# The entry of a fused attention backward loop: square root as a power on GpSimd, the last shift rows and the stores of q moved into the loop

## The chip, the cores and the metric

The kernel runs on one core of one Trainium2 chip. The metric is the device time of one execution in microseconds (us), as a median over runs. The core has five engines that run their own instruction queues in order and meet through semaphores: TensorE (PE, with PEld for its weight loads), VectorE (DVE), ScalarE (ACT), GpSimd (POOL) and SyncE (SP). TensorE writes to PSUM banks, which DVE and ACT read. DMAs are issued from the queues of SP, ACT and POOL.

## The reference

Two attention blocks over 2048 tokens and 448 columns, and the gradients of both. Block A is linear attention, block B is multi-query attention: 16 query heads of 28 columns share one key and one value head. Cut to block B, which the change concerns:

```python
q = (x @ wq).reshape(B, S, H, Dh).transpose(0, 2, 1, 3)
k = x @ wk
v = x @ wv
scores = jnp.einsum("bhqd,bkd->bhqk", q, k) * (Dh ** -0.5)
p = _softmax(scores, axis=-1)
o = jnp.einsum("bhqk,bkd->bhqd", p, v)
return o.transpose(0, 2, 1, 3).reshape(B, S, H * Dh) @ wo
```

The kernel returns the outputs of both blocks (concatenated) and the gradients of x and of all weights, for a given gradient of the output.

## The kernel before, in words

**Stages.** `phase_A` computes block A, forward and backward, until about 192 us. `phase_B_pre` then projects q, k and v of block B until about 218 us. The core, the loop `for u in range(NU + 28)`, computes block B's attention forward and backward together until about 1004 us. A tail computes the weight and input gradients that are left.

**phase_B_pre.** q is kept transposed in `R1`: four groups of 128 rows, in each four heads of 32 rows (28 columns of q and 4 more), 2048 tokens along the row. Row 0 of each head's 32 rows holds a shift, by which the softmax is kept from overflowing: the square root of |q|² times the largest |k|². It multiplies a row of −1 in k, so the product of q and k gives the shifted score at once. The loop over `qc` (four chunks of 512 tokens) makes, per chunk, four groups of q (ScalarE copies them out of PSUM, L585; DVE squares them, L587), a product that sums the squares by head into one PSUM bank `pn` (16 rows), a `Sqrt` of that bank on ScalarE with the scale `kmax2` (L592), and four small DMAs from POOL's queue that put the 16 rows into `R1` (L594, here called puts). After every second chunk four DMA transposes on SP (L599) bring 1024 tokens of q into the order of tokens, and one DMA (L600, 1 MB) stores them to `qn_d` in DRAM, from where the core loads them as `qX` for its dk products.

**The core.** There are 64 blocks: 256 query tokens by two heads each. A block takes 8 units, and a unit u is 256 keys of one block. Unit u does, each with its own lag:

- the scores of unit u on TensorE (into the banks `SB`, three in rotation) and the dp products of unit u−16 (banks `DB`), `rows_SD`;
- two exps of the scores on ScalarE (L904, L944) into the exp tiles `eT`, and from unit 16 on ScalarE's copy `cp` of the second dp half (L911), DVE's product of the first (L909), POOL's product of the second (L912);
- after every fourth unit one DMA transpose of an exp tile (`eN`, 1 MB, L946) on SP; the dv products (`dv_mm`, u−20) read it. Block 0's dv products in unit 20 need the first two eN tiles, block 1's in unit 28 the next two;
- on even units the o and dq products (`o_dq`), on odd units the dk products (`dk_m`, u−27), which read `qX`;
- once per block a normalisation of o: unit 10 of the block has `prod`, `don` and a copy on POOL (L800 to L804), which TensorE transposes in unit 14 (`don_T`).

**The order of the work.** The core is written under a manual schedule: each engine's instructions stand in program order. Outside of it a scheduler may reorder. `do_proj` projects the gradient of the output through wo, 16 tiles of 128 tokens in two halves of 256 columns each. The table `do_slots` (L881) says in which unit which half is made: units 1 to 15 (into the `DB` banks, which are free until unit 16, with four products of 128x256), five odd units 17 to 25 (into `dk_acc`, free until unit 27), and every eighth unit from 32 to 120 (into a spare `SB` bank). Outside the `DB` banks each half is made of 16 products of 32 columns each. `do_copy` copies a half out on DVE (L879).

**PSUM and SBUF.** `phase_A` and `phase_B_pre` use one PSUM pool of eight banks (`aacc` and `agen`, four each); the core opens another. The core's SBUF pools lie in the memory that the pools of `phase_A` held, so the first writes of the core wait for the last readers there. The shift rows of the first three chunks lie in such memory (`ga`), the fourth in `R3`, which stays.

**Activation tables.** ScalarE holds one table of functions at a time. `Sqrt` and `Exp` are not in the same one: the program loads a table ahead of the first L592 and one ahead of a dummy exp of one column, `ex` (L883), at the head of the core.

Of the kernel before, what the change touches and what calls it, by code (L numbers as in the profile page):

```python
# [8 lines left out]
ACT = mybir.ActivationFunctionType  # L9
# [5 lines left out]
H = 16  # L15
DH = 28
D = 448
P = 128
# [7 lines left out]
def kernel(  # L26
# [50 lines left out]
    ex = cst.tile([P, 1], F32, name="ex")  # L77
    nc.vector.memset(ex[:], 0.0)
# [9 lines left out]
    def flat(t):  # L88
        return t.rearrange("p a b -> p (a b)")
# [34 lines left out]
    def phase_A(pa, cA, cB, awk, psA):  # L124
# [401 lines left out]
        return xbT, wq_pad, rep, bsel, gaB, ga[:, 8:12, :]  # L526

    def phase_B_pre(pa, cA, awk, psA, io):
        xbT, wq_pad, rep, bsel, qn, sh = io
# [41 lines left out]
        shifts = [flat(sh)[0:H, i * 512:(i + 1) * 512] for i in range(NQC - 1)] + [flat(R3)[0:H, 5120:5632]]  # L571
        kmax2 = cA.tile([H, 1], F32, name="kmax2")
        for qc in range(NQC):
# [17 lines left out]
            shift = shifts[qc]  # L591
            nc.scalar.activation(out=shift, in_=pn[0:H, :], func=ACT.Sqrt, scale=kmax2[:, 0:1])  # L592
            for g in range(4):
                nc.gpsimd.dma_start(qT[:, g, qs].rearrange("(j r) s -> j r s", r=32)[:, 0, :], shift[4 * g:4 * g + 4, :])  # L594
            if qc % 2:
                q2 = slice((qc - 1) * 512, (qc + 1) * 512)
                t2 = slice(4 * qc - 4, 4 * qc + 4)
                for g in range(4):
                    nc.sync.dma_start_transpose(qn[:, t2, g * P:(g + 1) * P], qT[:, g, q2])  # L599
                nc.sync.dma_start(qn_d[q2, :].rearrange("(t p) c -> p t c", p=P), qn[:, t2, :])  # L600
# [5 lines left out]
        nc.gpsimd.memset(vaug_[:, :, 0:1], 1.0)  # L606

# [3 lines left out]
    kn_ = R3f[:, 4608:5120].rearrange("p (t c) -> p t c", c=32)  # L611
    with ExitStack() as pa:
        psA = pa.enter_context(tc.tile_pool(name="psA", bufs=4, space=bass.MemoryType.PSUM))
# [4 lines left out]
        phase_B_pre(pa, cA, awk, psA, io)  # L618
# [5 lines left out]
    psc = ExitStack()  # L624
    with ExitStack() as cs_:
        psA = psc.enter_context(tc.tile_pool(name="psAcc", bufs=1, space=bass.MemoryType.PSUM))
# [9 lines left out]
        SB = [psA.tile([P, 512], F32, name=f"sps{i}") for i in range(3)]  # L636
        DB = [psA.tile([P, 512], F32, name=f"dps{i}") for i in range(2)]
        oq = psA.tile([P, 512], F32, name="oq")
        dv_acc = psA.tile([P, 512], F32, name="dv_acc")
        dk_acc = psA.tile([P, 512], F32, name="dk_acc")  # L640
# [220 lines left out]
        def dv_mm(b, h, qb):  # L861
# [6 lines left out]
        def do_proj(i, h, ps):  # L868
            if ps is DB[0] or ps is DB[1]:
                for c in range(4):  # L870
                    mm(ps[:, 0:256], gbT[:, i, c, :], woTp[:, c, h * 256:(h + 1) * 256], start=(c == 0), stop=(c == 3))
                return
            for c in range(4):
                for j in range(4):
                    js = slice(32 * j, 32 * j + 32)
                    mmt(ps[js, 0:256], gbT[:, i, c, js], woTp[:, c, h * 256:(h + 1) * 256], (0, 32 * j), c == 0, c == 3)

        def do_copy(i, h, ps):
            nc.vector.tensor_copy(out=do_nat[:, i, h * 256:(h + 1) * 256], in_=ps[:, 0:256])  # L879

        do_slots = {u: divmod(n, 2) for n, u in enumerate([*range(1, 16), *range(17, 27, 2), *range(32, 128, 8)])}  # L881
        with tc.manual_schedule():
            tc.keep_in_program_order(nc.scalar.activation(out=ex[:], in_=ex[:], func=ACT.Exp))  # L883
            for u in range(NU + 28):
# [14 lines left out]
                if dpj is not None:  # L899
                    dps_ = DB[u % 2] if u < 16 else dk_acc if u < 27 else spare  # L900
                    do_proj(*dpj, dps_)
# [189 lines left out]
```

## Time and profile before

Three runs took 1079.1, 1080.79 and 1082.69 us, a median of 1080.79. The profiled execution took 1080.88 us, with a span of 1079.1 us between its first and last instruction.

| engine | busy us of the span | share |
|---|---|---|
| TensorE (PE) | 1027.6 | 95% |
| DVE | 895.5 | 83% |
| ScalarE (ACT) | 876.7 | 81% |
| POOL | 772.1 | 72% |

| what | count | one, in us |
|---|---|---|
| exp of the scores, ACT L904 and L944 | 1024 | 0.61 to 0.63 |
| copy `cp`, ACT L911 | 512 | 0.61 |
| product of 128x512, POOL L912 | 512 | 1.16 |
| square root of 16x512, ACT L592 | 4 | 0.68 |
| put of 4 shift rows, POOL L594 (issue; landing) | 16 | 0.56; 1.9 and 2.7 |
| q transposes, SP L599 (issue) | 8 | 1.2 to 2.8 |
| load of qX, POOL (issue; landing) | 32 | 0.6; 4.3 |

A busy time is the sum over instructions of an engine. Start to start, two exps lie 0.49 us apart, less than their duration, since neighbours overlap. "x4" in a timeline merges four instructions that follow each other. A value in square brackets is the idle time of the engine just before an instruction, and behind the arrow is what ended it. DMA shares can be over 1, as they add what the packets of all queues took on the 16 DMA engines.

### The profile page before, as it was taken

What the parts mean: (1) busy time and instruction counts of PE and PEld (TensorE: products, weight loads), DVE (VectorE), ACT (ScalarE), POOL (GpSimd) and SP (SyncE); (2) the same over time, 40 slices, a digit from 0 to 9 for tenths busy, and PEclk for the clock granted to TensorE, in tenths of its full rate; (3) what the DMA queues carried; (4) which work ended last, traced back from release to release, by engine and by line L of the source; (5) the groups of instructions that cost most, each with busy time, mean ns of one, the idle gap of its engine ahead of it and who ended that gap; (6) DMA issues with size and microseconds to landing.
All of it is one profiled execution on the core that took longest, in us unless ns stands there. A gap on an engine that the chain in (4) does not pass through costs nothing.

```text
span 1079.1 us, 40135 instructions
## 1 busy us (share of the span) xinstructions
PE 1027.6 (95%) x16326; PEld 489.1 (45%) x16329; DVE 895.5 (83%) x1792; ACT 876.7 (81%) x1744; POOL 772.1 (72%) x1014
## 2 busy tenths in 40 slices
PE   9999999998999999999999999999999999999998
PEld 5555455443444444444444444444444444444434
DVE  7897400447999999999999999999999999999943
ACT  6463122577999999999999999999999999999622
POOL 6001243327888888888988888988998899888881
PEclk9999999998999999999999999999999999999999
DMA  9979899499999999999999999999999999999973
GB/s 239 165 131 195 161 196 193 88 215 169 202 210 198 179 190 187 197 188 201 183 187 191 201 188 194 204 184 182 193 203 186 193 194 193 196 177 180 221 140 92
DMA packets 669026, 199.36 MB, mean 185 GB/s; under 512 B 646008, under 2 KB 664736, under 8 KB 668840
## 3 DMA queue, kind: packets, MB, share of 16 engines
q1 hardware_dynamic: 656296, 175.23, 95.5%
q0 software_dynamic: 7584, 17.59, 6.9%
q10 hardware_dynamic: 4960, 3.96, 1.4%
q8 instruction: 128, 2.10, 0.8%
q14 instruction: 58, 0.48, 0.2%
HBM read 20.99 MB, written 12.94 MB: 31 GB/s over the span
## 4 chain that ended last, share of the span: by engine, by line
PE 34%; POOL 18%; ACT 18%; DVE 14%; issue 12%; DMA 4%; DVEq 0%; ACTq 0%; POOLq 0%; SPq 0%
POOL dsT L912 13%; PE agen L81 13%; ACT cp L911 9%; ACT eT L944 7%; DVE dsx L975 6%; PE sps L653 5%; PE aacc L81 4%; PE oq L653 4%; DVE dsT L909 3%; DMA eN<-eT 2%; PE dv_acc L653 2%; POOL prod L800 1%; PE dps L653 1%; DMA out_dram<-dsT 1%; DVE R L929 1%
## 5 line engine op out<-in xcount | busy, mean ns | idle before, releaser
L912 POOL TENSOR_TENSOR dsT<-cp,eT 128x512 bf16<-128x512 bf16 x512 | 588.4, 1157 | 104.5 <-ACT cp L911 98.6
L975 DVE STREAM_TRANSPOSE dsx<-dsT 128x512 f32<-128x512 f32 x512 | 357.7, 699 | 2.3 <-DVE R L723 0.2
L653 PEld LDWEIGHTS <-R 128*32 128x32 bf16 (+1 forms) x9184 | 229.5, 94 | 278.8 <-issue 238.7
L909 DVE TENSOR_TENSOR dsT<-dps,eT 128x512 bf16<-128x512 f32 x512 | 341.6, 667 | 16.5 <-PE dps L653 11.7
L904 ACT ACTIVATE eT<-sps 128x512 bf16<-128x512 f32 x512 | 312.6, 611 | 22.9 <-PE dps L653 10.7
L911 ACT ACTIVATE cp<-dps 128x512 bf16<-128x512 f32 x512 | 314.2, 614 | 12.0 <-PE dps L653 10.9
L944 ACT ACTIVATE eT<-sps 128x512 bf16<-128x512 f32 x512 | 320.3, 626 | 0.0
L653 PE MATMUL dk_acc<-dsx,qX 32*32 32x512 bf16 x4096 | 268.3, 376 | 0.0
L653 PE MATMUL dps<-doT,R 32*128 32x256 bf16 x2048 | 248.7, 270 | 1.9 <-ACT cp L911 0.8
L653 PE MATMUL sps<-R,R 32*128 32x256 bf16 (+1 forms) x2240 | 222.1, 274 | 7.6 <-DVE R L879 1.7
L653 PE MATMUL oq<-eT,R 128*32 128x256 bf16 x2048 | 158.3, 275 | 1.4 <-issue 1.4
L653 PE MATMUL oq<-dsT,R 128*32 128x256 bf16 x2048 | 157.1, 275 | 0.1
L653 PEld LDWEIGHTS <-qX 32*32 32x32 bf16 x4096 | 79.8, 89 | 114.4 <-issue 54.1
L653 PE MATMUL dv_acc<-eN,don 128*32 128x512 bf16 x1024 | 98.1, 381 | 3.8 <-DMA eN<-eT 3.8
L81 PEld LDWEIGHTS <-R 128*128 128x128 bf16 (+1 forms) x525 | 41.5, 98 | 41.7 <-issue 12.2
L406 POOL COPY pk<-R 128x256 bf16<-128x256 bf16 x4 | 1.6, 399 | 73.2 <-DVE R L366 73.1
L653 PEld LDWEIGHTS <-don 128*32 128x32 bf16 x1024 | 33.8, 97 | 5.0 <-issue 4.5
L422 DVE TENSOR_TENSOR osb<-aacc,pr 64x448 bf16<-64x448 f32 x2 | 1.2, 616 | 41.1 <-ACT pr L421 24.9
L800 POOL TENSOR_TENSOR prod<-R,oTs 128x128 f32<-128x128 bf16 x64 | 28.0, 438 | 7.7 <-DVE oTs L796 7.4
L929 DVE TENSOR_SCALAR R<-oq 64x256 bf16<-64x256 f32 x64 | 27.3, 427 | 3.6 <-PE oq L653 1.6
L817 PE MATMUL sps<-identB,don 128*32 128x128 bf16 x256 | 18.6, 224 | 12.3 <-POOL don L809 8.4
L81 PE MATMUL agen<-R,R 128*128 128x448 bf16 x128 | 28.6, 352 | 0.0
(232 smaller groups left out, 978.7 us busy)
## 6 DMA issues: line engine op xcount, KB each, us to landing
qX<-qn_d POOLq DMA_DIRECT2D x32, 256.0 KB, 4.3
out_dram<-osb ACTq DMA_DIRECT2D x22, 112.0 KB
qn_d<-gaT SPq DMA_DIRECT2D x2, 1024.0 KB
eN<-eT SPq DMA_TRANSPOSE x128
xa<-in_A_x_dram SPq DMA_DIRECT2D x8, 224.0 KB
ga<-in_grad_out_dram SPq DMA_DIRECT2D x4, 448.0 KB
xa<-in_grad_out_dram POOLq DMA_DIRECT2D x4, 448.0 KB, 12.2
out_dram<-wdq POOLq DMA_DIRECT2D x8, 224.0 KB, 6.3
```

What stands on the lines that cost most here:

```text
L81: nc.tensor.matmul(out_ap, lhsT=lhsT, rhs=rhs, start=start, stop=stop, tile_position=(0, 0))
L406: nc.gpsimd.tensor_copy(out=pk[:, t4, D:512], in_=gqn[:, t4, 3 * P:D])
L653: nc.tensor.matmul(out, lhsT=lhsT, rhs=rhs, start=start, stop=stop, tile_position=pos, skip_group_check=True)
L800: nc.gpsimd.tensor_tensor(out=prod[b][:], in0=dnv, in1=os_, op=ALU.mult)
L817: nc.tensor.transpose(tp2[q:q + 32, qb * P:(qb + 1) * P], don[b][:, qb, h, :], identB[:, :], tile_position=(0, q))
L904: nc.scalar.activation(out=eT(u)[:, 0, :], in_=sp[0][:, :], func=ACT.Exp, scale=scale)
L909: nc.vector.tensor_tensor(out=dst[:, 0, :], in0=dp[0][:, :], in1=ew[:, 0, :], op=ALU.mult)
L911: nc.scalar.activation(out=cp[:, :], in_=dp[1][:, :], func=ACT.Copy)
L912: nc.gpsimd.tensor_tensor(out=dst[:, 1, :], in0=cp[:, :], in1=ew[:, 1, :], op=ALU.mult)
L929: nc.vector.tensor_scalar(out=qT_B[g][64 * hp:64 * hp + 64, qc * 256:(qc + 1) * 256], in0=oq[64:128, 0:256], scalar1=scale, scalar2=None, ...
L944: nc.scalar.activation(out=eT(u)[:, 1, :], in_=sp[1][:, :], func=ACT.Exp, scale=scale)
L975: nc.vector.transpose(out=dsx[b][:, tp, :, :, :].rearrange("p h t c -> p (h t c)").bitcast(F32), in_=dsT[y][:, :, :].rearrange("p h c -> p ...
```

## The change

Four things are changed.

1. The square root: a new function `q_shift` scales the sums with an `Identity` on ScalarE (`kmax2`, and 1e-30 added) into a temporary, and raises that to the power 0.5 with a `tensor_tensor` on POOL. The dummy exp is gone. All three calls in `phase_B_pre` use the same temporary, `tmp[0]`.
2. `phase_B_pre` makes the shifts of the chunks 0 to 2 and puts those of 0 and 1. The fourth `q_shift` and the puts of the chunks 2 and 3 stand in the core after the first exp of unit 1. The second four q transposes stand at the core's head, ahead of these puts, so q goes to `qn_d` without its shift rows for the last 1024 tokens; the dk rows that these make are not used. Their 1 MB store from SP becomes four stores of 256 tokens (256 KB) from POOL, in units 34, 42, 50 and 58. The loads of `qX` for the second chunk of 256 tokens move to units 66 to 78, and the load of `wo` from unit 70 to 86.
3. The core's PSUM banks are tiles of the pool of `phase_A` (`aacc`, `agen`); the bank of the fourth sum stays in use until unit 1 and then becomes `dv_acc`.
4. `do_proj` makes 13 whole tiles of 512 columns with four products each in the odd units 1 to 25, and six halves in the units 32 to 72.

```diff
+    def q_shift(pn, shift, tmp):
+        a = tmp[0][0:H, :]
+        nc.scalar.activation(out=a, in_=pn[0:H, :], func=ACT.Identity, bias=eps[:, 0:1], scale=kmax2[:, 0:1])
+        nc.gpsimd.tensor_tensor(out=shift, in0=a, in1=half[:, 0:1].to_broadcast([H, 512]), op=ALU.pow)
+
+    def put_shift(shift, qs):
+        for g in range(4):
+            nc.gpsimd.dma_start(R1[:, g, qs].rearrange("(j r) s -> j r s", r=32)[:, 0, :], shift[4 * g:4 * g + 4, :])
...
-            shift = shifts[qc]
-            nc.scalar.activation(out=shift, in_=pn[0:H, :], func=ACT.Sqrt, scale=kmax2[:, 0:1])
-            for g in range(4):
-                nc.gpsimd.dma_start(qT[:, g, qs].rearrange("(j r) s -> j r s", r=32)[:, 0, :], shift[4 * g:4 * g + 4, :])
-            if qc % 2:
-                q2 = slice((qc - 1) * 512, (qc + 1) * 512)
-                t2 = slice(4 * qc - 4, 4 * qc + 4)
+            if qc == NQC - 1:
+                break
+            q_shift(pn, shifts[qc], tmp)
+            if qc < 2:
+                put_shift(shifts[qc], qs)
+            if qc == 1:
                 for g in range(4):
-                    nc.sync.dma_start_transpose(qn[:, t2, g * P:(g + 1) * P], qT[:, g, q2])
-                nc.sync.dma_start(qn_d[q2, :].rearrange("(t p) c -> p t c", p=P), qn[:, t2, :])
+                    nc.sync.dma_start_transpose(qn[:, :, g * P:(g + 1) * P], qT[:, g, 0:1024])
+                nc.sync.dma_start(qn_d[0:1024, :].rearrange("(t p) c -> p t c", p=P), qn)
...
-        SB = [psA.tile([P, 512], F32, name=f"sps{i}") for i in range(3)]
-        DB = [psA.tile([P, 512], F32, name=f"dps{i}") for i in range(2)]
-        oq = psA.tile([P, 512], F32, name="oq")
-        dv_acc = psA.tile([P, 512], F32, name="dv_acc")
-        dk_acc = psA.tile([P, 512], F32, name="dk_acc")
+        SB = [psA.tile([P, 512], F32, name="aacc") for i in range(3)]
+        DB = [psA.tile([P, 512], F32, name="agen") for i in range(2)]
+        oq, dk_acc = (psA.tile([P, 512], F32, name="agen") for _ in range(2))
...
-        do_slots = {u: divmod(n, 2) for n, u in enumerate([*range(1, 16), *range(17, 27, 2), *range(32, 128, 8)])}
+        do_slots = {2 * i + 1: (i, 0, 512) for i in range(13)}
+        do_slots.update({32 + 8 * n: (13 + n // 2, n % 2 * 256, n % 2 * 256 + 256) for n in range(6)})
         with tc.manual_schedule():
-            tc.keep_in_program_order(nc.scalar.activation(out=ex[:], in_=ex[:], func=ACT.Exp))
+            qn = pqa_.tile([P, 8, 512], BF16, name="qX")
+            for g in range(4):
+                nc.sync.dma_start_transpose(qn[:, :, g * P:(g + 1) * P], R1[:, g, 1024:2048])
...
                 if hasS:
                     nc.scalar.activation(out=eT(u)[:, 0, :], in_=sp[0][:, :], func=ACT.Exp, scale=scale)
+                if u == 1:
+                    q_shift(pn3, shifts[3], [pd_.tile([P, 2, 512], BF16, name="dsT").rearrange("p a b -> p (a b)").bitcast(F32)
+                                             for _ in range(1)])
+                    for qc in (2, 3):
+                        put_shift(shifts[qc], slice(qc * 512, qc * 512 + 512))
+                    dv_acc = psA.tile([P, 512], F32, name="aacc")
...
+                for n in {34: (0,), 42: (1,), 50: (2,), 58: (3,)}.get(u, ()):
+                    nc.gpsimd.dma_start(qn_d[1024 + 256 * n:1280 + 256 * n, :].rearrange("(t p) c -> p t c", p=P),
+                                        qn[:, 2 * n:2 * n + 2, :])
...
-                if u == 70:
+                if u == 86:
                     nc.gpsimd.dma_start(wo, wo_d[:, 0:D].rearrange("(g p) c -> p g c", p=P))
```

## The prediction

> **What bounds the kernel now.** I read the granted clock first (0.995, one core, nothing to correct), then the busy shares in stretches of 10 us, the chain of waits, and last the timelines of ScalarE, of SP's queue and of TensorE where the fused attention loop ("core", from 219 us) begins. The columns of the stretches are busy us per engine (PE, weight loads, DVE, ACT, POOL), clock, DMA share, GB/s.
>
> ```profile
> 200.00:210.00 10.00, 9.89 (x46) 4.20 (x45) 4.62 (x12) 7.10 (x12) 2.29 (x4) 1.00 0.01 2
> 230.00:240.00 10.00, 9.77 (x94) 5.02 (x94) 4.41 (x14) 8.21 (x16) 1.83 (x5) 1.00 1.09 262
> 240.00:250.00 10.00, 8.33 (x128) 4.12 (x127) 7.57 (x16) 8.59 (x18) 6.30 (x9) 0.99 1.20 152
> 260.00:270.00 10.00, 7.28 (x126) 2.94 (x120) 6.59 (x14) 6.33 (x13) 5.89 (x9) 0.85 1.21 226
> 330.00:412.00 82.00, 78.05 (x1534) 37.21 (x1532) 78.93 (x152) 80.14 (x160) 70.91 (x85) 1.00 1.08 189
> 412.00:1003.00 591.00, 567.76 (x11150) 263.42 (x11142) 576.33 (x1119) 584.16 (x1171) 522.07 (x621) 1.00 1.13 191
> ```
>
> Before the core TensorE alone is full. From 412 us on ScalarE is 98.8% busy (584.16 of 591) and nothing in this change touches it there. Between them, at 240 to 270 us, no engine is full and the DMA share is over 1.1. The chain says who is late:
>
> ```profile
> 216.51 3.62 DMA R<-ga
> 220.40 0.20 ACT ex L883
> 236.06 13.86 DMA eN<-eT
> 249.97 1.04 PE dv_acc L653 x6
> 256.13 9.73 DMA eN<-eT
> ```
>
> The entry waits for the shift rows' third put and for `ex`; then two transposes of exp tiles (eN) hold TensorE's dv products. ScalarE's and SP's timelines give the causes:
>
> ```profile
> 204.10 1.28 ACT L592 ACT_TABLE_LOAD   x1
> 218.41 0.68 ACT L592 ACTIVATE R<-aacc,kmax 16x512 bf16<-16x512 f32 x1 [0.93 <-PE aacc L81]
> 219.10 1.28 ACT L883 ACT_TABLE_LOAD   x1
> 220.51 0.58 ACT L904 ACTIVATE eT<-sps 128x512 bf16<-128x512 f32 x1
> 251.58 0.60 ACT L904 ACTIVATE eT<-sps 128x512 bf16<-128x512 f32 x1 [2.18 <-PE dps L653]
> 266.88 0.60 ACT L904 ACTIVATE eT<-sps 128x512 bf16<-128x512 f32 x1 [2.60 <-PE dps L653]
> ```
>
> ```profile
> 212.47 5.94 SPq L599 DMA_TRANSPOSE gaT<-R  x4
> 220.64 0.36 SPq L600 DMA_DIRECT2D qn_d<-gaT  x1
> 221.16 8.80 SPq L599 DMA_TRANSPOSE gaT<-R  x4
> 230.07 5.32 SPq L946 DMA_TRANSPOSE eN<-eT  x1
> 235.55 0.46 SPq L600 DMA_DIRECT2D qn_d<-gaT  x1
> 236.06 26.12 SPq L946 DMA_TRANSPOSE eN<-eT  x3
> ```
>
> SP works in order. The first exp tile could leave when unit 3's exps are done (226 us) but leaves at 230.07, behind the second four q transposes, which lay 2.8 us longer than the first four because they waited for the last shift's put; the second store of q (1 MB) then stands ahead of the second exp tile. Counting units of the core by their first exp: unit 16 starts at 241.84, a usual unit takes 1.45 to 1.6 us, unit 20 takes 3.78 and unit 28 takes 4.20.
>
> **What the Trainium skill says.** "ScalarE: Activation LUTs", sections on the cost of ACT_TABLE_LOAD and on table sets: exp and square root are in different sets, identity and copy in all of them; a load is 1283 ns and a drain of 1380 ns. Two loads of 1.28 us are in the trace; the 1.38 us are not (the load at 204.10 follows an ACTIVATE that ended at 204.09). "GPSIMD Engine Reference", section 3.1: a two-input elementwise loop takes 2.6 cycles an element; the trace has 1157 ns for the product of 512 elements (L912), the same within 5%. The page also gives about 12 cycles an element for branching on data and about 3 operations a cycle for longer bodies, but prices no power. "DMA: Bandwidth & Descriptors", "Issuing engines are not separate DMA queues": all queues share 16 engines and interleave. The trace agrees: the share is over 1 while three queues run.
>
> **The change, part by part.** p is the time of one 16x512 power on POOL; no row shows it.
>
> *Tables.* Both loads and `ex` go. The first load is free: TensorE was busy 9.89 of 10 us beside it. The second is on the entry. TensorE's last product before the core ends at 218.49; its first scores waited 0.79 us for DVE (L605) through the change of PSUM pools, which goes as well. Scores at 218.5 and an exp at 218.95 instead of 220.51: gain 1.55.
>
> *Power chain.* First sum of squares at 204.97, scaling on ACT 0.7, power from 206.0 to 206+p, four puts of 0.56 (2.24, L594) to 208.3+p. The second scaling (ready 209.8) reuses the first one's temporary, so it waits for the power: free while p is under 3.8. Second power from 210.7 (POOL free if p is under 2.4) to 210.7+p, its puts land near 215+p. The first exp waits for these puts (their rows lie in reused memory; before, it waited for the third put at 220.14): free while p is under about 4. The third power has no puts behind it. The fourth follows a scaling between unit 1's exps (ACT +0.7 there).
>
> What is p? Below: not under 1.16, the product of the same length. Above: a logarithm, a product and an exponential at an assumed 60 operations and the page's 3 a cycle is 20 cycles an element, 8.5 us, an estimate from "GPSIMD Engine Reference". I take 2: straight-line code, since the program lifts zero by 1e-30 and so leaves no special case for the power to catch. This is a choice, not a reading.
>
> *SP.* The first q transposes wait for the second puts: start 212.4+p instead of 212.47, store 220.6+p, second transposes 221.1+p. These now stand ahead of the last puts in the program and wait for no put, so they take 6.0: first exp tile at 227.1+p. The second store is gone from SP (0.5 with its gaps); the second exp tile at 232.6+p, before 236.06.
>
> *DMA.* From 220.64 to the fourth exp tile's landing at 265.9, eight MB pass (two stores, four q transposes, four exp tiles at 1 MB, four loads of 0.25): 45.3 us, 5.65 us per MB. Taking one MB away moves the landings earlier by 5.65, and the later start takes p back: 5.65−p = 3.65. TensorE could use up to 8.1 (1.55 entry, 0.8 below, 5.75 of stalls at units 20, 28 and 29), so DMA still sets the pace: gain 3.65 over the whole stretch to unit 31, the entry's included.
>
> *Projection tiles.* Units 1 to 15: 15 halves at 0.54 become 8 whole tiles at 0.87 (four 128x512 products, as the q projection takes): −1.1, less 0.3 for ACT's scaling: −0.8. Units 17 to 25: five halves at 0.62 become five whole tiles, TensorE +1.25, DVE +1.3 (0.68 against 0.42 a copy). The DMA waits hide this: DVE is at 7.57 of 10. Without that cover it costs up to 1.3. Six halves of units 80 to 120 go: ACT is at 97.7% in 330:412 against 98.8% later, which bounds the gain at 0.7 over these 60 us; I take 0.5.
>
> *Moved stores and loads.* Four stores of 256 KB on POOL in units 34 to 58 take the places of four equal loads, which move to 66 to 78, and wo's load to 86. POOL issues each in about 0.6 (the load's row) and is 88% busy: four more make 2.4 us over 44 units, in gaps; the rows are wanted at unit 91. Taken as 0, up to 0.5 if POOL's products are late.
>
> *Last puts.* POOL's eight puts wait for the second q transposes to land (229 to 231+p), then 2.8 and a load's issue 0.6 stand ahead of block 0's `prod`: 233 to 234.5+p, where 232.7 is wanted and the later transpose on TensorE leaves 2.1 of slack. With p=2 a stall of 0.2 to 1.7 near unit 14, which then shortens the DMA stall at unit 20: 0 in the sum.
>
> Sum: −3.65−0.5 = −4.15 on the profiled execution's own 1080.88 (span 1079.1), near the median 1080.79: **1076.7**.
>
> **Rivals.**
> *Slow power (slower).* Place: POOL before the core. The second puts end at 210.6+2p and land 2 later, so the first exp moves by 2p−7.9 against before, and the third scaling waiting on POOL holds ScalarE's copies and TensorE. It decides from p of about 4.5. At 8.5: entry +9.1; puts and `prod` late once more, +2; of the later stalls about 2 come back: +9, 1090. At 5.1 (12 cycles an element, an estimate from the same page) the entry is +2.3 and the sum +2: 1083. For it: a power is several steps, and four sit on one queue. Against: 16 partitions of short vectors, and the 2.7 cycles of the product.
> *Hidden store (no change).* The issue of the transposes (5.3 us each) sets the landings, not the bytes. Then the second exp tile is only 3.4−p = 1.4 earlier: 1079.0 with the 0.5. For it: the issue of an exp tile takes 5.6 in the median between 220 and 340 us, near the 5.65 of a MB. Against: the three from 236.06 took 8.7 each, longer than an issue that nothing holds up (5.32 for the first).
> *All stalls go.* The spaced loads and the missing store free more than a mean MB: 8.1+0.5, 1072.3. Against: share 1.2 at 240 to 270.
> *Not as said.* The built program has no load of a table left but the first, so this part holds.
>
> **How the numbers follow.** Chances: forecast 0.45 (own range 1074.5 to 1078.5), all stalls go 0.07, hidden store 0.20, slow power 0.28 (1081 to 1095). The range 1073 to 1088 leaves out most of the 0.07 and the slow tail, about 0.15. 0.3% is 3.2 us, what a measurement can tell: faster 0.39+0.07+0.01 = 0.47; same 0.06+0.18+0.02 = 0.26; slower 0.26, and 0.01 of the hidden store, 0.27.
>
> **What would show it.** Power rows on POOL near 2 us; first exp near 219; the first exp tile's transpose on SP at about 229 with no store behind it; unit 20 no longer over 3 us. Wrong if a power takes over 4 us, if ScalarE's scaling waits on POOL, or if dv still waits 2 us for eN.

## The result: 28% slower

The changed kernel takes 1385.48 us (median of 4 runs, 1384.4 to 1387.25) against 1081.05 (1079.1 to 1082.69): a ratio of 1.282, interval 1.279 to 1.284. The forecast was 1076.7 in a range of 1073 to 1088, so the time lies far outside it, on the other side of no change. The profiled execution of the changed kernel has a span of 1383.4 us, 304.3 more than before.

The page of the changed kernel, parts 1, 2 and 4 (busy us and shares; busy tenths in 40 slices of 34.6 us each; the chain of waits by engine):

```profile
span 1383.4 us, 39752 instructions
PE 1032.4 (75%) x16145; PEld 484.6 (35%) x16145; DVE 895.5 (65%) x1780; ACT 874.1 (63%) x1741; POOL 1101.5 (80%) x1022
...
PE   9999990010100502899999999999999999999998
...
POOL 4012529999999998888888888888988988888882
PEclk9999995555555655999999999999999999999999
...
POOL 32%; PE 26%; issue 17%; ACT 15%; DVE 9%; DMA 0%; DVEq 0%; ACTq 0%; POOLq 0%
```

The busy time of TensorE, DVE and ScalarE is within 5 us of before; only POOL's grew, from 772.1 to 1101.5. In the nine slices from about 208 to 519 us POOL alone is full; TensorE, busy for 95% of the span before, works for half of one of them and hardly at all in the others. POOL's timeline (start, duration, engine, line, operation, tiles; in brackets the idle time before and its cause) says what it does there:

```profile
204.70 81.97 POOL L613 TENSOR_TENSOR ga<-gaT,half 16x512 bf16<-16x512 f32 x1 [11.03 <-ACT gaT L612]
286.96 2.35 POOL L617 DMA_DIRECT2D R<-ga  x4 [0.29 <-POOL ga L613]
289.33 81.96 POOL L613 TENSOR_TENSOR ga<-gaT,half 16x512 bf16<-16x512 f32 x1
371.58 2.30 POOL L617 DMA_DIRECT2D R<-ga  x4 [0.29 <-POOL ga L613]
373.95 81.95 POOL L613 TENSOR_TENSOR R<-gaT,half 16x512 bf16<-16x512 f32 x1
...
456.49 0.16 POOL L607 MEMSET R<- 128x16 bf16 x1
457.02 81.92 POOL L613 TENSOR_TENSOR R<-dsT,half 16x512 bf16<-16x512 f32 x1 [0.37 <-issue]
538.91 4.53 POOL L617 DMA_DIRECT2D R<-R  x8
543.43 0.59 POOL L937 DMA_DIRECT2D qX<-qn_d  x1
544.04 0.44 POOL L808 TENSOR_TENSOR prod<-R,oTs 128x128 f32<-128x128 bf16 x1
```

One power takes 82 us. The four follow each other with nothing but the puts, a few fills of constants and gaps of up to 0.4 us between them: 81.97 + 81.96 + 81.95 + 81.92 = 327.8 us. Block 0's `prod` stands behind all of it on POOL's queue and starts at 544.04. Before, by POOL's timeline, it started at 234.78 and waited for DVE:

```profile
234.78 0.43 POOL L800 TENSOR_TENSOR prod<-R,oTs 128x128 f32<-128x128 bf16 x1 [7.38 <-DVE oTs L796]
```

That is 309.3 later now; the other 18.5 us of the powers fill time that POOL had spent waiting there. From `prod` to the end of the span the changed kernel takes 839.4 us against 844.3 before, 5.0 less. 309.3 − 5.0 is the whole difference of 304.3.

What the other engines waited for, from part 5 of the same page (busy and mean ns of a group, then its idle time and what ended it):

```profile
L661 PE MATMUL agen<-eT,R 128*32 128x256 bf16 x2048 | 159.4, 277 | 76.6 <-POOL R L607 76.6
...
L612 ACT ACTIVATE gaT<-aacc,eps,kmax 16x512 f32<-16x512 f32 x3 | 2.3, 771 | 159.6 <-POOL ga L613 158.7
...
L825 PE MATMUL aacc<-identB,don 128*32 128x128 bf16 x256 | 18.6, 224 | 84.8 <-POOL don L817 81.1
```

Three places, one cause. ScalarE's second and third scaling wait for the power ahead of them, as all three share one temporary (158.7 us in two waits). TensorE's o products of unit 2 wait 76.6 us for a 0.16 us memset (L607, the column of ones in `vaug`), which stands on POOL behind the third power. Its transposes of `don` in unit 14 wait for the fourth. ScalarE's timeline shows the same from the side of the exps:

```profile
286.70 0.77 ACT L612 ACTIVATE gaT<-aacc,eps,kmax 16x512 f32<-16x512 f32 x1 [78.76 <-POOL ga L613]
...
371.32 0.77 ACT L612 ACTIVATE gaT<-aacc,eps,kmax 16x512 f32<-16x512 f32 x1 [79.94 <-POOL ga L613]
...
377.80 0.60 ACT L914 ACTIVATE eT<-aacc 128x512 bf16<-128x512 f32 x1 [1.79 <-PE aacc L661]
...
458.32 0.60 ACT L914 ACTIVATE eT<-aacc 128x512 bf16<-128x512 f32 x1 [76.87 <-PE aacc L661]
```

The first exp comes at 377.80 instead of 220.51, and the core stops after three units (0 to 2) until 458.32.

### The profile page after: what moved, and what is told of

It reads as the page before. It is cut to its first block, busy times and chain, and to the rows that moved or that the text cites. A ratio compares the mean times of both kernels' runs of the same rounds, so it can differ in the third digit from the quotient of the medians.

```text
span 1383.4 us, 39752 instructions
## 1 busy us (share of the span) xinstructions
PE 1032.4 (75%) x16145; PEld 484.6 (35%) x16145; DVE 895.5 (65%) x1780; ACT 874.1 (63%) x1741; POOL 1101.5 (80%) x1022
## 4 chain that ended last, share of the span: by engine, by line
POOL 32%; PE 26%; issue 17%; ACT 15%; DVE 9%; DMA 0%; DVEq 0%; ACTq 0%; POOLq 0%
POOL R L613 12%; POOL dsT L928 9%; ACT cp L927 8%; PE agen L84 7%; POOL ga L613 6%; ACT eT L964 6%; PE agen L661 6%; PE aacc L661 5%; PE aacc L84 5%; DVE dsx L995 3%; DVE dsT L925 2%; POOL prod L808 1%; POOL don L811 1%; PE aacc L825 1%; ACT eT L914 1%
## 5 line engine op out<-in xcount | busy, mean ns | idle before, releaser
L914 ACT ACTIVATE eT<-aacc 128x512 bf16<-128x512 f32 x512 | 312.6, 611 | 170.0 <-PE aacc L661 155.4
L925 DVE TENSOR_TENSOR dsT<-agen,eT 128x512 bf16<-128x512 f32 x512 | 341.9, 668 | 12.2 <-PE agen L661 7.3
L661 PEld LDWEIGHTS <-R 32*128 32x128 bf16 (+1 forms) x9008 | 224.2, 94 | 357.1 <-issue 242.3
L927 ACT ACTIVATE cp<-agen 128x512 bf16<-128x512 f32 x512 | 314.2, 614 | 12.3 <-PE agen L661 11.0
L964 ACT ACTIVATE eT<-aacc 128x512 bf16<-128x512 f32 x512 | 320.3, 626 | 0.0
L661 PE MATMUL agen<-dsx,qX 32*32 32x512 bf16 x4096 | 267.9, 375 | 0.0
L661 PE MATMUL agen<-doT,R 32*128 32x256 bf16 x2048 | 248.8, 270 | 4.4 <-DVE dsT L925 1.8
L661 PE MATMUL aacc<-R,R 32*128 32x256 bf16 (+1 forms) x2144 | 219.6, 275 | 5.8 <-DVE doT L832 1.0
L661 PE MATMUL agen<-eT,R 128*32 128x256 bf16 x2048 | 159.4, 277 | 76.6 <-POOL R L607 76.6
L613 POOL TENSOR_TENSOR ga<-gaT,half 16x512 bf16<-16x512 f32 x2 | 163.9, 81962 | 11.1 <-ACT gaT L612 11.0
L661 PE MATMUL agen<-dsT,R 128*32 128x256 bf16 x2048 | 156.5, 274 | 0.1
L612 ACT ACTIVATE gaT<-aacc,eps,kmax 16x512 f32<-16x512 f32 x3 | 2.3, 771 | 159.6 <-POOL ga L613 158.7
L613 POOL TENSOR_TENSOR R<-dsT,half 16x512 bf16<-16x512 f32 x1 | 81.9, 81917 | 0.4 <-issue 0.4
```

Of the source, the lines that this page charges most:

```text
L613: nc.gpsimd.tensor_tensor(out=shift, in0=a, in1=half[:, 0:1].to_broadcast([H, 512]), op=ALU.pow)
L661: nc.tensor.matmul(out, lhsT=lhsT, rhs=rhs, start=start, stop=stop, tile_position=pos, skip_group_check=True)
L914: nc.scalar.activation(out=eT(u)[:, 0, :], in_=sp[0][:, :], func=ACT.Exp, scale=scale)
L925: nc.vector.tensor_tensor(out=dst[:, 0, :], in0=dp[0][:, :], in1=ew[:, 0, :], op=ALU.mult)
L927: nc.scalar.activation(out=cp[:, :], in_=dp[1][:, :], func=ACT.Copy)
L964: nc.scalar.activation(out=eT(u)[:, 1, :], in_=sp[1][:, :], func=ACT.Exp, scale=scale)
```

## The experiments

Two questions were put to the chip: is the duration of the power the whole cause, and of what kind is that duration; and what is the rest of the change worth without it. Ratios are to the kernel before, run on the same chip in between.

### The power by itself, and a quarter of it

The kernel before with six GpSimd instructions at its end, on constant data (2.0, and 0.5 as the exponent; the text below says seven, but names the six):

```diff
+        hb = lambda p_, n_: h[0:p_, 0:1].to_broadcast([p_, n_])
+        nc.gpsimd.tensor_tensor(out=outs_["a"][0:16, 0:512], in0=x[0:16, 0:512], in1=hb(16, 512), op=ALU.pow)
+        nc.gpsimd.tensor_tensor(out=outs_["b"][0:16, 0:128], in0=x[0:16, 0:128], in1=hb(16, 128), op=ALU.pow)
+        nc.gpsimd.tensor_tensor(out=outs_["c"][0:128, 0:64], in0=x[0:128, 0:64], in1=hb(128, 64), op=ALU.pow)
+        nc.gpsimd.tensor_tensor(out=outs_["d"][0:1, 0:512], in0=x[0:1, 0:512], in1=hb(1, 512), op=ALU.pow)
+        nc.gpsimd.tensor_tensor(out=outs_["g"][0:16, 0:512], in0=x[0:16, 0:512], in1=hb(16, 512), op=ALU.mult)
+        nc.gpsimd.tensor_tensor(out=outs_["k"][0:16, 0:512], in0=x[0:16, 0:512], in1=h[0:16, 0:512], op=ALU.pow)
```

> The kernel before with seven POOL instructions added after its end, on tiles of their own, of constant data: powers of 16x512 (za), 16x128 (zb), 128x64 (zc), 1x512 (zd), 16x512 with a full tile as exponent (zk), and a product of 16x512 (zg). If the cost goes by columns[...]: 82, 20.5, 10.2, 82, 82 us, product 1.2. If by elements per core, lane by lane: 82, 20.5, 10.2, 5.1, 82. If by elements over all cores in series: zc is 82. If constant data take a short way: all shorter than 82. A broadcast exponent being the slow part would show as zk far below za.

One run took 1360.84 us. The groups of instructions of that kernel at its end, where the tile `za` is the output "a" of the edit and so on (line, tiles and shapes, count; busy us and mean ns; idle time before):

```profile
L1076 POOL TENSOR_TENSOR zk<-zx,zh 16x512 bf16<-16x512 f32 x1 | 82.1, 82127 | 0.0
L1071 POOL TENSOR_TENSOR za<-zx,zh 16x512 bf16<-16x512 f32 x1 | 82.0, 81968 | 9.1 <-issue 9.1
L1074 POOL TENSOR_TENSOR zd<-zx,zh 1x512 bf16<-1x512 f32 x1 | 81.9, 81907 | 0.0
L1072 POOL TENSOR_TENSOR zb<-zx,zh 16x128 bf16<-16x128 f32 x1 | 20.7, 20715 | 0.0
L1073 POOL TENSOR_TENSOR zc<-zx,zh 128x64 bf16<-128x64 f32 x1 | 10.5, 10505 | 0.0
...
L1075 POOL TENSOR_TENSOR zg<-zx,zh 16x512 bf16<-16x512 f32 x1 | 1.0, 1029 | 0.0
```

The price is that of the columns: 512 columns cost 82 us on 16 partitions and on one, 128 cost 20.7, 64 cost 10.5 on all 128. From 20.7 to 82.0 it is 61.25 us for 384 columns, 160 ns each. Nothing about the exponent's broadcast counts: a whole tile of exponents (zk) takes the same. The product of the same shape takes 1.03, one eightieth.

The changed kernel with the power on the first 128 columns of each chunk; the other 384 are copied, so their root is left out:

```diff
-        nc.gpsimd.tensor_tensor(out=shift, in0=a, in1=half[:, 0:1].to_broadcast([H, 512]), op=ALU.pow)
+        nc.gpsimd.tensor_tensor(out=shift[:, 0:128], in0=a[:, 0:128], in1=half[:, 0:1].to_broadcast([H, 128]), op=ALU.pow)
+        nc.gpsimd.tensor_copy(out=shift[:, 128:512], in_=a[:, 128:512])
```

> The changed kernel with the power on 128 of the 512 columns; the other 384 columns are left without a root (copied on POOL). Theory A (time per element, in series on POOL): a power takes 20.5 us, block 0's prod comes near 300 us instead of 544, and the run takes about 1141 us (1385 less 4 x 61.4, with 0.4 for each copy). Rival (a fixed cost of the instruction[...]): a power stays near 82 us and the run near 1385.

One run took 1142.0 us, against 1385.48: 243.5 less. POOL's timeline of that kernel, first and last of its powers, and `prod`:

```profile
206.28 20.77 POOL L613 TENSOR_TENSOR ga<-gaT,half 16x128 bf16<-16x128 f32 x1 [11.03 <-ACT gaT L612]
...
276.41 20.72 POOL L613 TENSOR_TENSOR R<-dsT,half 16x128 bf16<-16x128 f32 x1 [0.37 <-issue]
...
302.68 0.44 POOL L809 TENSOR_TENSOR prod<-R,oTs 128x128 f32<-128x128 bf16 x1
```

Its four powers take 83.0 us, 244.8 less than the full ones, and `prod` starts 241.4 earlier. So a microsecond taken from the powers is, but for half a per cent, a microsecond of the whole.

### The memset behind the third power

The wait of 76.6 us on a memset looks like something to mend. It was given to DVE:

```diff
-        nc.gpsimd.memset(vaug_[:, :, 0:1], 1.0)
+        nc.vector.memset(vaug_[:, :, 0:1], 1.0)
```

> The changed kernel (four powers on POOL), but the ones column of vaug is set by DVE instead of POOL, so it no longer stands behind the third power. Theory A (the o products' 76.6 us wait for it lies beside the fourth power; block 0's product for the normalisation, behind all four powers on POOL, sets the end): 1383 to 1386, no change. Theory B (the waits of TensorE add up): about 1309, 76 less.

1387.55 us (2 runs): no gain. TensorE's timeline of that kernel between 370 and 560 us, two of its waits:

```profile
458.24 0.47 PE L794 MATMUL aacc<-identF,oTs 64*128 64x64 f32 x2 [66.66 <-POOL identF masks.py:199]
...
547.08 0.29 PE L825 MATMUL aacc<-identB,don 128*32 128x128 bf16 x2 [80.64 <-POOL don L817]
```

The o products no longer wait. Eight units on, the core stops all the same, 66.66 us, for the identity matrix `identF`, which POOL fills behind the third power too; and then 80.64 us for the normalisation behind the fourth. So the run did not take the wait on the third power away, it moved it by some units. What decides is on POOL: the fourth power starts 0.48 us after the fill, without waiting for TensorE, and `prod` follows the fourth power (545.70, with the first power 1.6 us later than in the changed kernel). Nothing that TensorE does earlier can bring that forward.

### The change without the power

*No root at all.* One Identity on ScalarE gives 0.5x + 0.5 instead of the root of x; no table load is left on the entry. (`kmax2` is halved by a small DVE instruction where it is made.) Everything else of the change stays.

```diff
-        a = tmp[0][0:H, :]
-        nc.scalar.activation(out=a, in_=pn[0:H, :], func=ACT.Identity, bias=eps[:, 0:1], scale=kmax2[:, 0:1])
-        nc.gpsimd.tensor_tensor(out=shift, in0=a, in1=half[:, 0:1].to_broadcast([H, 512]), op=ALU.pow)
+        nc.scalar.activation(out=shift, in_=pn[0:H, :], func=ACT.Identity, bias=half[:, 0:1], scale=kmax2[:, 0:1])
```

> Here the shift is computed otherwise: 0.5*x + 0.5 in place of the square root of x (never below it, so the softmax is still kept from overflowing), by the one Identity on ScalarE that the changed kernel has already; the power on POOL is gone, and nothing else of the change is touched. Theory A (the four powers of 82 us in series are the whole loss, the rest of the change is a small gain): 1073 to 1080 us, first exp near 219 us, units 20 and 28 each under 2.5 us. Theory B (another part costs as well: the banks shared with the earlier pool, the transposes at the core's head, or the moved stores): over 1084 us, with a wait of more than 3 us on one of these in the trace.

*The root back on ScalarE*, all four ahead of the core, with the table load and the dummy exp on the entry as before:

```diff
-            if qc == NQC - 1:
-                break
             q_shift(pn, shifts[qc], tmp)
...
+        nc.scalar.activation(out=shift, in_=pn[0:H, :], func=ACT.Sqrt, scale=kmax2[:, 0:1])
...
+            tc.keep_in_program_order(nc.scalar.activation(out=ex[:], in_=ex[:], func=ACT.Exp))
...
-                    q_shift(pn3, shifts[3], [pd_.tile([P, 2, 512], BF16, name="dsT").rearrange("p a b -> p (a b)").bitcast(F32)
-                                             for _ in range(1)])
```

> The changed kernel with only the square root put back on ScalarE (Sqrt from PSUM, all four ahead of the core, both table loads and the dummy exp back). Theory A: 1075 to 1082 us, some 1.5 us above e1_linear, the price of the second table load at the core's entry. Theory B: over 1084 us here too. If the loads were hidden after all: equal to e1_linear within 0.5 us.

The linear version took 1080.94 us (22 runs, 1071.9 to 1091.7; ratio 1.0004, interval 0.998 to 1.002). The root on ScalarE took 1074.18 (9 runs, 1072.9 to 1077.5; ratio 0.9946, 0.993 to 0.996), although it keeps the table load. Both expectations missed: the linear version should have been a little faster than before, and the root on ScalarE 1.5 us slower than the linear one; it is 6.8 us faster. Whether that was luck, and whether the place of the fourth scaling held the linear version back, was asked next. The linear version with the fourth ahead of the core:

> The version with a linear shift (no root: 0.5x+0.5 by one Identity on ScalarE, no table loads), but with the fourth scaling ahead of the core, as all four are where the square root is back on ScalarE. It leaves the root out. Theory A (the fourth scaling between unit 1's exps, and the bank it holds, is what kept the linear version at 1080.9 with runs from 1072 to 1092): 1073 to 1075 with runs within 5 us. Theory B (the entry that starts earlier without the table loads runs into the DMA of the exp tiles, wherever the fourth scaling is): again near 1081 with runs 10 us or more apart.

and the root on ScalarE once more:

> The version with the square root back on ScalarE once more, in other runs, beside the next kernel. Theory A (its gain is real: store out of the entry and whole tiles together): ratio to before 0.993 to 0.997, 1073 to 1077. Theory B (the 1074.18 was a lucky set of 9 runs; runs of these kernels lie 5 to 13 us apart): within 0.3% of before.

The first gave 1080.23 (22 runs, 1074.4 to 1090.2; 0.9998, 0.998 to 1.002), the second 1074.09 (6 runs, 1072.8 to 1076.7; 0.995, 0.993 to 0.997). So the gain is real. The earlier entry, without a table load, buys nothing, with the fourth scaling in either place.

The parts taken away one by one: the projection tiles in halves again, in the version with the root on ScalarE,

```diff
...
-        do_slots = {2 * i + 1: (i, 0, 512) for i in range(13)}
-        do_slots.update({32 + 8 * n: (13 + n // 2, n % 2 * 256, n % 2 * 256 + 256) for n in range(6)})
+        do_slots = {u: (n // 2, n % 2 * 256, n % 2 * 256 + 256) for n, u in enumerate([*range(1, 16), *range(17, 27, 2), *range(32, 128, 8)])}
...
```

> The version with the square root back on ScalarE (1074.18 us, ratio to before 0.9946), but with the projection tiles in halves as before (15 in units 1 to 15, five in 17 to 25, twenty in all from 32 on every eighth unit). Theory A (the store of q that left the entry is worth most of the 5.9 us; the tiles are worth what the prediction's sum gave them, 1.1 in units 1 to 15 and 0.5 later, less what five whole tiles in units 17 to 25 cost): 1075 to 1076. Theory B (the tiles are worth most, as the DMA stalls at unit 20 come anyway): 1078 to 1080.

the second store of q back on SP, behind its transposes,

```diff
+            nc.sync.dma_start(qn_d[1024:2048, :].rearrange("(t p) c -> p t c", p=P), qn)
             for u in range(NU + 28):
...
-                for n in {34: (0,), 42: (1,), 50: (2,), 58: (3,)}.get(u, ()):
-                    nc.gpsimd.dma_start(qn_d[1024 + 256 * n:1280 + 256 * n, :].rearrange("(t p) c -> p t c", p=P),
-                                        qn[:, 2 * n:2 * n + 2, :])
```

> The version with the square root back on ScalarE, but with the second store of q (1 MB) on SP directly behind its four transposes, ahead of the second exp tile's, and without the four spaced stores of units 34 to 58. Theory A (a MB in the entry sets the landings of the exp tiles, 5.65 us each): 1078 to 1080. Theory B (the store is hidden: the issue of the transposes sets the landings): 1074 to 1075.

and the whole tiles alone, put into the kernel before (the reverse of the first of these two edits):

> The kernel before with the whole projection tiles alone (do_slots and do_proj of the changed kernel); entry, stores and PSUM pools as before. Theory A (the tiles are worth 1.3 to 1.6 us by the prediction's sum): 1079 to 1080. Theory B (the tiles carry most of the 5.9 us, as taking them out again cost about 8): 1074 to 1076. Theory C (the two help only together): 1080 to 1082.

The halves took 1082.87 us (22 runs, 1075.4 to 1088.7; ratio 1.0023, 1.0003 to 1.0043), slower than either theory had it. The store on SP took 1077.44 (14 runs, 1072.3 to 1085.6; 0.9982, 0.9961 to 1.0002), between the two. The tiles alone took 1079.61 (14 runs; 0.9988, 0.9968 to 1.0007): no change that can be measured. The parts don't add up: neither pays alone, together they give 0.995. The starts of the units show where the time went in one execution of each. The table is worked out from the first exps of the units in ScalarE's timelines. A row is no median: the one of the root on ScalarE, again, is the fastest of its six runs (1072.78), the one of the tiles alone the slowest but one of its 14 (1083.26).

| kernel | unit 0 at | 0 to 16 | 16 to 32 | 32 to 64 | 64 to 511 | longest unit from 16 to 32 |
|---|---|---|---|---|---|---|
| before | 220.51 | 21.33 | 30.57 | 51.31 | 679.46 | 4.20 |
| changed | 377.80 | 171.60 | 27.64 | 50.54 | 679.43 | none over 2.4 |
| root on ScalarE, again | 218.96 | 20.50 | 26.67 | 50.67 | 679.42 | none over 2.4 |
| linear, fourth ahead | 218.43 | 19.26 | 32.76 | 50.63 | 679.35 | 7.60 |
| tiles alone | 221.61 | 24.37 | 32.28 | 49.87 | 677.55 | 5.88 |
| halves again | 219.46 | 25.22 | 26.29 | 50.76 | 687.33 | 2.63 |
| store on SP again | 221.21 | 21.75 | 26.36 | 49.29 | 678.50 | none over 2.4 |

The linear version with the fourth ahead is 4.2 us earlier than before at unit 16 (237.69 against 241.84) and has 2.0 of it left at unit 32. Its view of waits between 250 and 275 us (total, count, longest), and then a piece of its chain of waits there (start, length):

```profile
PEld L658 <- DMA qX<-qn_d: 5.1, 1, 5.1
```

```profile
249.71 12.09 DMA qX<-qn_d
```

Unit 27 has the first dk products, and they need the fourth quarter of `qX`, issued on POOL in unit 22. It took 12.09 us to land, at 261.80; before, the same load was issued at 255.35 and took 5.43, to 260.79. So the units ahead of it came earlier, and the load did not land earlier. Why it took longer is not shown. (The first linear version was profiled in the slowest of its 22 runs, 1091.66 us, which can't stand for the others.) With the root on ScalarE almost nothing waits; the view of the tile `qX` in its second set of runs (issues: lowest, median and highest ns, first and last start; then the us that TensorE waited and the us to landing):

```profile
L934 POOL DMA_DIRECT2D qX<-qn_d x4: 576/580/616, 230.7 to 251.5; - x4
...
  DMA qX<-qn_d: 0.4, 1
DMA to landing us min/median/max: 3.4/5.2/7.4
```

Its last quarter is issued at 251.5 and landed by 258.9 at the latest; unit 27 starts at 258.46. There is no slack in it. So a few microseconds more in one landing are enough for a wait. That such waits make the runs of one version lie 9 to 20 us apart is not shown: the halves again and the store on SP again have none from unit 16 to 32 in their profiles, and their runs lie 13 us apart too.

### Two steps further

The column 32 to 64 holds one more thing. With four spaced stores on POOL these 32 units take 50.67 us; with the store on SP, and none there, 49.29. So the stores were moved to SP, in their spaced places:

```diff
-                    nc.gpsimd.dma_start(qn_d[1024 + 256 * n:1280 + 256 * n, :].rearrange("(t p) c -> p t c", p=P),
+                    nc.sync.dma_start(qn_d[1024 + 256 * n:1280 + 256 * n, :].rearrange("(t p) c -> p t c", p=P),
                                         qn[:, 2 * n:2 * n + 2, :])
```

> The version with the square root back on ScalarE (1074.1 us, ratio 0.995), with its four spaced stores of 256 KB (units 34 to 58) issued from SP instead of POOL. In the profiled runs units 32 to 64 took 50.67 us with the stores on POOL and 49.29 without them. Theory A (their issue on POOL, ahead of products that DVE waits for, costs 1.4): units 32 to 64 in about 49.3, 1072 to 1073.5. Theory B (their bytes cost it, wherever they are issued): 50.7 again, 1074 to 1075.

1072.27 us (6 runs, 1070.5 to 1073.3; ratio 0.9911, 0.988 to 0.994), with 49.28 us from unit 32 to 64, the size that theory A gave. Nine profiled kernels with the stores on POOL take 50.5 to 50.8 there; this one and the store on SP again take 49.3. But it is TensorE that waits, not DVE. With the stores on POOL (the root on ScalarE, again), POOL's timeline has a store's issue right ahead of `prod`:

```profile
271.67 0.78 POOL L927 DMA_DIRECT2D qn_d<-qX  x1
272.47 0.45 POOL L806 TENSOR_TENSOR prod<-R,oTs 128x128 f32<-128x128 bf16 x1
```

So `don` comes late, and its transposes on TensorE and their weight loads wait for it. The views of waits over these 32 units, first with the stores on POOL:

```profile
PEld L823 <- POOL don L815: 3.1, 4, 0.8
PE aacc L823 <- POOL don L815: 1.9, 4, 0.5
```

With the stores on SP:

```profile
PEld L823 <- POOL don L815: 0.4, 2, 0.2
```

There is a second cost, 400 units later. In all nine kernels with the stores on POOL, and in none of the other four, POOL stands still for 1.3 us ahead of the last load of `qX`, and the transposes of unit 446 are late again. POOL's timelines, with the stores on POOL and on SP:

```profile
892.93 0.59 POOL L934 DMA_DIRECT2D qX<-qn_d  x1 [1.30 <-issue]
```

```profile
893.22 0.57 POOL L934 DMA_DIRECT2D qX<-qn_d  x1
```

Units 440 to 448 take 13.52 us in the first and 12.14 in the second. What POOL waits for, the trace does not name. Of all versions tried the one with the stores on SP has the lowest median and ratio; its interval just touches that of the same version with the stores on POOL (0.993 to 0.997).

And DVE: from unit 16 to 32, where the forecast had hidden five whole tiles behind transfers, the stretches of before and of the version with the root on ScalarE (busy us of PE, weight loads, DVE, ACT, POOL; clock, DMA share, GB/s):

```profile
241.84:272.41 30.57, 25.78 (x412) 11.24 (x410) 23.64 (x47) 24.28 (x49) 21.01 (x26) 0.89 1.21 176
```

```profile
239.46:266.13 26.67, 22.77 (x347) 10.23 (x349) 25.04 (x47) 24.22 (x49) 20.95 (x26) 1.00 1.23 204
```

DVE is at 94% of the shorter stretch (25.04 of 26.67). So halves were put back there alone:

```diff
-        do_slots = {2 * i + 1: (i, 0, 512) for i in range(13)}
-        do_slots.update({32 + 8 * n: (13 + n // 2, n % 2 * 256, n % 2 * 256 + 256) for n in range(6)})
+        do_slots = {2 * i + 1: (i, 0, 512) for i in range(8)}
+        do_slots.update({u: (8 + n // 2, n % 2 * 256, n % 2 * 256 + 256) for n, u in enumerate([*range(17, 27, 2), *range(32, 120, 8)])})
```

> The version with the square root back on ScalarE, with whole tiles in the units 1 to 15 only; units 17 to 25 make halves as the kernel before does, and the other eleven halves stand from unit 32 to 112. In the profiled runs units 16 to 32 took 26.67 us with DVE busy in 25.04 of them, so the five whole tiles' copies (1.3 us more on DVE) are no longer hidden there. Theory A (DVE bounds this stretch now): units 16 to 32 in about 25.4, and up to 0.6 back later for five more halves, 1073 to 1074. Theory B (the transfers still bound it): 26.4 to 26.7 again, 1074.5 to 1075.5.

Both theories missed: 1079.69 us (14 runs, 1072.9 to 1084.0; ratio 0.9991, 0.9964 to 1.0017), with 32.84 us from unit 16 to 32, of which unit 27 alone took 8.64. Its view of waits between 240 and 330 us, and a piece of its chain:

```profile
PEld L659 <- DMA qX<-qn_d: 6.2, 1, 6.2
```

```profile
253.36 11.74 DMA qX<-qn_d
```

Units 16 to 25 did run faster, 15.42 us against 16.62, the 1.2 that DVE was to give. Then the load of `qX` was not there. Of its wait the faster units explain at most these 1.2 us. The larger part is the load itself: it took 11.74 us, where the fourth quarter took 7.37 in the version with whole tiles. So in this execution the slower stretch had covered a little of the load; why the load took longer is not shown.

## Why the prediction was wrong

**The step that failed is the size of p.** "Above: ... an assumed 60 operations ... 8.5 us" and "I take 2": measured 81.95, forty times the value taken and 9.6 times the upper bound. The upper bound took the 3 operations a cycle of longer bodies from the Trainium skill ("GPSIMD Engine Reference", section 3.1) and divided a count by it that no row showed; at the page's rate and clock the measured time would be some 580 operations a column, an estimate, not 60. The product of the same shape, 2 ns a column (1.03 us for 512), is no neighbour of 160 ns. So the bound was an assumption, and the range up to 1088 stood on it. The value of 2 rested on "straight-line code", which nothing showed either.

**The rival had the mechanism.** "Slow power" named the place (POOL before the core). Its formula puts the first exp 2p − 7.9 later; at p = 81.95 that is 156.0, and it came 157.3 later (377.80 against 220.51). It too was mis-sized by its p. It also priced what follows wrongly: "puts and `prod` late once more, +2" for the third and fourth power. `prod` stands behind all four on POOL, so the shift is 4p less what POOL had idled, 327.8 − 18.5. With the quarter power the same count gives 83.0 − 18.5 = 64.5, and `prod` came 67.9 later (302.68 against 234.78); four copies of 0.49 that were added make 2.0 of the difference. Had the queue been written down to `prod`, the rival would have grown as 4p, by the same count (an estimate) to 15.5 us at its own p of 8.5 instead of 9. The memset of `vaug` and the fill of `identF` behind the third power were overlooked; they stop TensorE early, but have no price while `prod` is behind the fourth.

**The signs** were well chosen: a power over 4 us and ScalarE's scaling waiting on POOL were named as what would make it wrong, and both are there. The third, dv waiting for eN, is not in the changed kernel: no unit from 16 to 32 takes over 2.4 us.

**The rest of the sum**, which the changed kernel hides, is not confirmed. The version nearest to the forecast's kernel is the first linear one: no table load on the entry, the fourth scaling in unit 1, and no power at all. The sum gives it 4.15 or more, and no gain came (ratio 1.0004). The root on ScalarE, which keeps the table load, gained 5.4 to 5.8 us (ratios 0.995 and 0.9946). That this lies near 4.15 is in part luck, as the terms show. Sizes are from the profiled execution of the root on ScalarE, again, against that of before:

- *DMA and the stalls* (−3.65): 16 to 32 went from 30.57 to 26.67, −3.90, and units 20 and 28 are no longer over 3 us. Even the changed kernel has −2.93 there. But the claim "Taking one MB away moves the landings earlier by 5.65" is not shown: with the store on SP again the profiled run, the second fastest of its 14, had no stall either (26.36), while its median was 3.4 us above (0.9982 against 0.995 of 1080.9), and the linear version with the fourth ahead has a stall of 7.60 without that MB. As far as the single profiles go, it matters whether eN and `qX` land before their units; what sets that is open.
- *Entry* (gain 1.55, inside the 3.65): right where the table load goes. From the end of TensorE's last product ahead of the core to the first exp it was 2.02 us before, and 0.63 in the linear version with the fourth ahead. Over its whole time that version gained nothing, so the entry was not what set the time, as "DMA still sets the pace" had it. With the table load kept it is 2.02 again: the 0.79 us through the change of PSUM pools went, but TensorE's next scores then wait longer for the exp. TensorE's timeline before, then with the root on ScalarE:

```profile
219.28 0.49 PE L653 MATMUL sps<-R,R 32*128 32x256 bf16 x5 [0.79 <-DVE R L605]
221.14 0.37 PE L653 MATMUL sps<-R,R 32*128 32x256 bf16 x3 [1.37 <-ACT eT L904]
```

```profile
216.87 0.49 PE L659 MATMUL aacc<-R,R 32*128 32x256 bf16 x5
219.59 0.57 PE L659 MATMUL aacc<-R,R 32*128 32x256 bf16 x3 [2.22 <-ACT eT L913]
```

  Its unit 0 is 1.55 us earlier in the table only because the work ahead of the entry ended 1.55 us earlier in that run; in the first profile of the same kernel it comes at 221.25, later than before. (Before has three table loads, not two: the one at 1.93 us is the one that stays.)
- *Tiles* (−0.8 in units 1 to 15, later −0.5): the first can't be read. 0 to 16 took 20.50 and 21.86 us in two profiles of the same kernel, with granted clocks of 0.85 and 0.66 from 220 to 230 us, and 24.37 with the tiles alone, against 21.33. The second was undersized: it stood for the halves that go from units 80 to 120, and units 80 to 128 went from 74.53 to 72.66, −1.87 (72.65 with the tiles alone). The bound of 0.7 taken from ScalarE's busy share did not hold. As a version of their own the tiles show no measurable change of the whole time.
- *Five whole tiles in units 17 to 25*, "the DMA waits hide this": they did while those waits were there. Where they are gone, units 16 to 25 take 1.2 us more than with halves.
- *Moved stores and loads* ("0, up to 0.5"): mis-sized. The stores on POOL cost 1.39 in units 32 to 64 against none there (50.67 − 49.28), and 0.80 against the loads whose places they took (49.87 with the tiles alone). The moved loads cost 0.33 in units 64 to 80 (24.96 against 24.63 with the tiles alone), and units 440 to 448 cost 1.36: 2.5 together. Of these, 1.7 lie past unit 64 and nearly cancel the 1.9 of the tiles, so 64 to 511 looks unchanged in the table. The 0.64 less from 32 to 64 is no gain of either: before has 3.27 us in unit 48, where the others have about 1.8.
- *SP's queue*: the second transposes take 7.2 instead of 6.0, and the first exp tile follows them directly. SP's timeline in that run:

```profile
218.36 7.24 SPq L892 DMA_TRANSPOSE qX<-R  x4
225.64 194.27 SPq L963 DMA_TRANSPOSE eN<-eT  x32
```

Open: from unit 64 on, the profiled execution of the halves again lost 8 us (687.33 against 679.42). Of these, 1.9 lie in units 80 to 128, where its halves stand. 5.3 lie in units 448 to 456, where TensorE is idle for 3.22 us at 911.80 with no wait that the trace names. That the load of `qX` decides between 1074 and 1080 is read from single traces; a version that loads it earlier was not tried. Nor was the change with the shifts spread over 128 partitions, where the power would cost 10.5 us for a chunk by the measured price.

## What to carry to other kernels

An operation that no row of the profile and no page prices is measured by itself before it goes ahead of anything: its price can be eighty times that of its neighbour in the same instruction form, and an upper bound made of assumed steps is no bound. For an engine that works in order, write its queue down to the first instruction that another engine waits for, and multiply: here four powers stood ahead of one `prod`. And where loads land with nothing to spare, faster work ahead of them may end in a wait: set each gain beside the slack of the load behind it. Last, a sum that comes out near the measured time proves none of its terms: here two of them were off in opposite directions.

## What the runs showed of the hardware that was not expected

- GpSimd's power costs 160 ns a column, whatever the number of partitions (81.9 us for 512 columns on 1 partition, 82.0 on 16; 10.5 for 64 columns on 128) and whether the exponent is broadcast or a tile.
- While TensorE stood idle, its granted clock fell to about half: 0.54 from 208 to 370 us, where it was busy for 8.8 of 162, and the whole span's mean fell from 0.995 to 0.885. This agrees with the Trainium skill ("TensorE: Matmul & The Clock Gate", Part 1), where the clock of an idle array is half of full speed; what the forecast had not thought of is that a wait on another engine brings it on.
- Four stores of 256 KB cost 1.4 us in their own 32 units when POOL issued them and nothing measurable there when SP did, with the same bytes in the same units (50.67 and 49.28 us). With them on POOL a later issue on its queue stood 1.3 us with no wait that the trace names, in nine profiled kernels of nine, and in none of the four without.
